# Loading a KV cache in 64 KB rows through one ring of ten units, on one Trainium2 core

## The chip, the core and the metric

The kernel runs on one core of a Trainium2 chip. The core has a matrix engine (TensorE, "PE" in the profile; "PEld" is its loading of weights), a vector engine (DVE), a scalar engine (ACT), a general engine (POOL) and a sync engine (SP), which here only issues DMAs and waits for semaphores. Sixteen DMA engines move data from the memory of the chip (HBM, "dram" in names) to the core's SBUF, which has 128 partitions. PE accumulates into a second memory, PSUM. The metric is the device time of one execution in microseconds.

Each engine runs its own list of instructions in order, and engines meet at semaphores: `wait_ge(s, n)` holds an engine's list until semaphore `s` has reached `n`. A DMA adds 16 to its semaphore, one for each of the sixteen DMA engines that took part, so it counts as landed when the last of them is done.

## The reference

One token passes through an attention block that reads a long KV cache, and through a small gated MLP; a gate mixes the two. Everything is bf16.

```python
H, Sk, Dh, D, F = 32, 65536, 128, 512, 1792
q = (x @ wq).reshape(H, Dh)                                   # x: [1, 512], wq: [512, 4096]
p = softmax(einsum("hd,hkd->hk", q, k_cache) * Dh ** -0.5)    # k_cache: [32, 65536, 128]
a = einsum("hk,hkd->hd", p, v_cache).reshape(1, H * Dh) @ wo  # wo: [4096, 512]
b = (silu(x @ w_gate) * (x @ w_up)) @ w_down                  # [512, 1792] twice, [1792, 512]
g = sigmoid(sum(x * gate_w))
out = g * a + (1 - g) * b
```

K and V are 512 MB each in this count of 1 MB = 2^20 bytes (the profile's MB are 10^6 bytes: 1087.67 with the weights). Each is read once, and there is next to no reuse.

## The kernel before, in words

**Units and tiles.** A head's K is cut into eight chunks of 8192 positions, 2 MB each; so is its V. A chunk fills one 16 KB slot of all 128 partitions: partition p gets 64 consecutive positions, one contiguous row of 16 KB in HBM (`kv_src`, line 145). There are 256 K chunks and 256 V chunks.

**K chunk, on DVE and PE.** DVE transposes the chunk in 32x32 blocks of 32-bit words from the ring into one of two buffers `kt` (line 269, semaphore `ktdone`), which frees the ring slot. PE then multiplies it with the head's query, spread out in `qd`: 64 small matmuls into `psS` (line 346, `qkdone`).

**Head turn.** After a head's eight K chunks DVE takes the maximum of the scores in each partition (line 275), POOL makes it one maximum over all partitions (line 201) and the bias of the exponential (line 203), ACT computes the exponentials and their sum (line 217, `expdone`), and DVE shuffles the result into `pb`, the layout that V needs, in sixteen copies (line 285, `s_pb`). These steps stand in DVE's list among the transposes of the next head: the maximum behind its first chunk, the shuffle behind its second.

**V chunk, on PE alone.** 64 matmuls accumulate a head's output in `psO` straight from the ring (line 363, `pvdone`), which frees the slot. After a head's last V chunk DVE normalises (line 292, `s_otn`) and PE projects the head with its slice of `wo` into `psY` (line 372). One projection stands in PE's list for each head, some chunks later.

**The order of the loads.** `ring_order` (lines 47 to 53) alternates K chunk j with V chunk j - 10, so ten K chunks come first and ten V chunks last. SP issues all loads in that order on one queue; slot n % 7 of the ring is used again when its last user is done (line 185). PE's list has the same order. The weights have tiles of their own, some of which share SBUF space with tiles of other stages: `wq` is loaded first (behind the two small rows of x and gate_w), `w_gate`, `w_up` and `w_down` after two K chunks, `wo` before the thirteenth ring load and after a wait for the MLP (line 181). In HBM, `wq` is read in rows of 8 KB, `w_gate` and `w_up` in 3.5 KB, `w_down` and `wo` in 1 KB.

**MLP.** PE does its first part behind the fourth K chunk (`mlp_up`, line 319) and the second behind the fifth (`mlp_down`, line 328); DVE's part (`mlp_steps`, line 252) stands behind the fifth transpose and holds DVE until PE's second part is done (line 259).

Of the kernel before, what the change touches and what calls it, by code (L numbers as in the profile page):

```python
# [5 lines left out]
P = 128  # L6
CK = 8192
RB = CK // P
NR = RB // 4
NS = 7  # L10
LAG = 10

ALU = mybir.AluOpType
# [3 lines left out]
U32 = mybir.dt.uint32  # L17
AX_X = mybir.AxisListType.X
RMAX = bass.bass_isa.ReduceOp.max
RADD = bass.bass_isa.ReduceOp.add  # L20


def bass_gated_mix__mha_block_cached__swiglu_ffn__decode_kernel(
# [18 lines left out]
    NCH = S // CK  # L42
    NT = H * NCH
    SCALE = float(Dh) ** -0.5
    assert Dh == 128 and D == 512 and F % P == 0 and NCH * RB == 512

    ring_order = []
    for j in range(NT):
        ring_order.append(("k", j))
        if j >= LAG:  # L50
            ring_order.append(("v", j - LAG))
    for j in range(NT - LAG, NT):
        ring_order.append(("v", j))
    slot = {}
    fill = {}
    for n, key in enumerate(ring_order):
        slot[key] = n % NS
        fill[key] = 16 * (n // NS + 1)

    with ExitStack() as ctx:  # L60
# [15 lines left out]

        sel = sb("sel", [P, 4, 128], BF16)
# [21 lines left out]
        ring = sb("ring", [P, NS, RB * Dh], BF16)  # L99

        s_x = sem("s_x")
        s_wq = sem("s_wq")
        s_w1 = sem("s_w1")
        s_wo = sem("s_wo")
        rs = [sem(f"rs{i}") for i in range(NS)]
# [33 lines left out]
        wq_dram = A_wq.rearrange("(c p) n -> p c n", p=P)  # L139
        wg_dram = B_w_gate.rearrange("(c p) f -> p c f", p=P)  # L140
        wu_dram = B_w_up.rearrange("(c p) f -> p c f", p=P)
        wd_dram = B_w_down.rearrange("(c p) n -> p c n", p=P)
        wo_dram = A_wo.rearrange("(h d) n -> d h n", d=Dh)

        def kv_src(kind, j):
            src = A_k_cache if kind == "k" else A_v_cache
            h, c = j // NCH, j % NCH
            return src[0, h, c * CK:(c + 1) * CK, :].rearrange("(p r) d -> p (r d)", p=P)

        with ExitStack() as early:  # L150
            wq_t = early.enter_context(nc.sbuf_tensor("wq_t", [P, Dc, H * Dh], BF16))
            wq_end = nc.sbuf_base
        kt = ctx.enter_context(nc.sbuf_tensor("kt", [P, 2, RB * Dh // 2], U32))
        assert nc.sbuf_base >= wq_end
        with ExitStack() as mlp:
            wg_t = mlp.enter_context(nc.sbuf_tensor("wg_t", [P, Dc, F], BF16))
            wu_t = mlp.enter_context(nc.sbuf_tensor("wu_t", [P, Dc, F], BF16))
            wd_t = mlp.enter_context(nc.sbuf_tensor("wd_t", [P, FC, D], BF16))
            mlp_end = nc.sbuf_base
        wo_t = ctx.enter_context(nc.sbuf_tensor("wo_t", [P, H, D], BF16))  # L160
        if nc.sbuf_base < mlp_end:
            ctx.enter_context(nc.sbuf_tensor("mlp_pad", [P, (mlp_end - nc.sbuf_base + 64) // 2], BF16))

        ktb = [kt[:, b, :].bitcast(BF16).rearrange("p (j r m e) -> p j r m e", j=2, r=NR, e=2) for b in range(2)]

        block = ctx.enter_context(nc.Block())
        MLP_AT = 2
        WO_AT = 12

        @block.sync  # L170
        def _(sp):
            sp.dma_start(xrow[0:1, :], xr_dram).then_inc(s_x, 16)
            sp.dma_start(gwrow[0:1, :], gw_dram).then_inc(s_x, 16)
            sp.dma_start(wq_t[:], wq_dram).then_inc(s_wq, 16)
            for n, (kind, j) in enumerate(ring_order):
                if n == MLP_AT:
                    sp.dma_start(wg_t[:], wg_dram).then_inc(s_w1, 16)
                    sp.dma_start(wu_t[:], wu_dram).then_inc(s_w1, 16)  # L178
                    sp.dma_start(wd_t[:], wd_dram).then_inc(s_w1, 16)  # L179
                if n == WO_AT:  # L180
                    sp.wait_ge(s_b, 1)
                    sp.dma_start(wo_t[:], wo_dram).then_inc(s_wo, 16)
                if n >= NS:
                    pkind, pj = ring_order[n - NS]
                    sp.wait_ge(ktdone if pkind == "k" else pvdone, pj + 1)
                sl = slot[(kind, j)]
                sp.dma_start(ring[:, sl, :], kv_src(kind, j)).then_inc(rs[sl], 16)  # L187
# [20 lines left out]
        def _(act):  # L208
# [12 lines left out]
            act.wait_ge(s_out, 16)  # L221

        @block.vector
        def _(dve):
# [37 lines left out]
            for i in range(NT + LAG + 16):  # L262
                if i < NT:
                    dve.wait_ge(rs[slot[("k", i)]], fill[("k", i)])
                    if i >= 2:
                        dve.wait_ge(qkdone, i - 1)
                    o = kt[:, i % 2, :].rearrange("p (j r t) -> p r j t", j=2, t=32)
                    src = ring[:, slot[("k", i)], :].bitcast(U32).rearrange("p (r j t) -> p r j t", j=2, t=32)
                    nc.vector.transpose(o, src).then_inc(ktdone, 1)  # L269
                if i == 4:  # L270
                    mlp_steps()
                if i % NCH == 0 and 0 <= i // NCH - 1 < H:
                    h = i // NCH - 1
                    dve.wait_ge(qkdone, NCH * (h + 1))
                    nc.vector.reduce_max(mxs[:, h:h + 1], psS[:, h % 2, :], AX_X).then_inc(s_mx, 1)  # L275
                if i % NCH == 1 and 0 <= i // NCH - 1 < H:
                    h = i // NCH - 1
                    dve.wait_ge(expdone, h + 1)
                    if h >= 2:
                        dve.wait_ge(pvdone, NCH * (h - 1))  # L280
                    for g in range(4):
                        for b in range(4):
                            dst = pb[32 * g:32 * g + 32, h % 2, :].rearrange("p (n b) -> p n b", b=4)[:, :, b]
                            sr = pa[32 * b:32 * b + 32, h % 2, :].rearrange("p (n g) -> p n g", g=4)[:, :, g]
                            last = nc.vector.tensor_copy(dst, sr)  # L285
                    last.then_inc(s_pb, 1)
                if i % NCH == 3 and 0 <= i // NCH - 2 < H:
                    h = i // NCH - 2
                    dve.wait_ge(s_L, h + 1)
                    link(nc.vector.reciprocal(Li[:, h:h + 1], Lt[:, h:h + 1]))  # L290
                    dve.wait_ge(pvdone, NCH * (h + 1))
                    nc.vector.tensor_scalar(oTn[:, h:h + 1], psO[:, h % 2, h:h + 1], Li[:, h:h + 1], None,  # L292
                                            ALU.mult).then_inc(s_otn, 1)
# [5 lines left out]
        def _(pe):  # L299
            pe.wait_ge(s_x, 32)  # L300
            pe.wait_ge(s_ones, 1)
            for c in range(Dc):
                last = nc.tensor.matmul(psM[:, c:c + 1], xrow[0:1, c * P:(c + 1) * P], ones1[0:1, 0:1],
                                        start=True, stop=True)
            last.then_inc(s_xT, 1)
            pe.wait_ge(s_xTb, 1)
            pe.wait_ge(s_wq, 16)
            for h in range(H):
                for c in range(Dc):
                    last = nc.tensor.matmul(psM[:, 128 + h:129 + h], wq_t[:, c, h * Dh:(h + 1) * Dh],  # L310
                                            xTb[:, c:c + 1], start=(c == 0), stop=(c == Dc - 1))
# [7 lines left out]
            def mlp_up():  # L319
                pe.wait_ge(s_w1, 48)  # L320
                for fc in range(FC):
                    for w, o in ((wg_t, 64), (wu_t, 80)):
                        for c in range(Dc):
                            last = nc.tensor.matmul(psM[:, o + fc:o + fc + 1], w[:, c, fc * P:(fc + 1) * P],  # L324
                                                    xTb[:, c:c + 1], start=(c == 0), stop=(c == Dc - 1))
                last.then_inc(s_h, 1)

            def mlp_down():
                pe.wait_ge(s_gu, 1)
                for fc in range(FC):  # L330
                    last = nc.tensor.matmul(psB[0:1, :], guT[:, fc:fc + 1], wd_t[:, fc, :],  # L331
                                            start=(fc == 0), stop=(fc == FC - 1))
                last.then_inc(s_b, 1)

            for i in range(NT + LAG + 16):
                if i < NT:
                    h, c = i // NCH, i % NCH
                    pe.wait_ge(ktdone, i + 1)
                    if i == 0:
                        pe.wait_ge(s_qd, 1)  # L340
                    if c == 0 and h >= 2:
                        pe.wait_ge(expdone, h - 1)
                    for r in range(NR):
                        col = c * RB + 4 * r
# [5 lines left out]
                if i == 3:  # L350
                    mlp_up()
                if i == 4:
                    mlp_down()
                if 0 <= i - LAG < NT:
                    v = i - LAG
                    h, c = v // NCH, v % NCH
                    if c == 0:
# [46 lines left out]
```

## Time and profile before

| | |
|---|---|
| median of three runs | 2604.55 us (2604.51 to 2605.13) |
| the profiled execution | 2604.43 us, of which its span, first to last instruction, 2602.6 us |
| HBM read | 1087.64 MB, 418 GB/s over the span |
| DMA, busy share of the sixteen engines | 99.1% for the queue of the loads, 0.7% for instructions |
| DVE transposes of K, line 269 | 256, 1137.5 us busy |
| PE on K, line 346, and on V, line 363 | 16384 matmuls each, 478.2 and 472.8 us busy |
| K and V DMAs from issue to landing, median | 31.2 and 29.9 us |

A row of the timeline has a start and a duration in us from the span's start, the engine, the line of the kernel, the operation, output and inputs, and how often; in brackets stands how long the engine had been idle before, and what ended that. "issue" means that the engine waited for nothing that the profile shows. A row of the windows has a stretch, its length, the busy time and the number of instructions of PE, PEld, DVE, ACT and POOL, then the granted clock of PE, the busy share of the sixteen DMA engines and the rate of all transfers. Besides these the trace holds one record for every DMA packet (queue, start, duration, size) and one for every DMA engine's landing of every DMA.

### The profile page before, as it was taken

To read this page: it belongs to the slowest core of one execution; us is meant where nothing else is said; L and a number is where in the kernel's file an instruction comes from. 1 tells how busy PE (TensorE), PEld (TensorE's weight loads), DVE (VectorE), ACT (ScalarE), POOL (GpSimd) and SP (SyncE) were. 2 spreads that over 40 slices of the span, in tenths; PEclk is the share of its full clock that TensorE was granted. 3 is DMA by queue.
4 is the path that set the end of the run, shared out by engine and by line. 5 is a ranking of instruction groups with operands and counts; after the bars stand their busy time and mean duration, and the time that the engine had idled before them with its cause. 6 is when DMAs were issued, how large, how long until landed. Compare 5 with 4: busy or idle time off the path is not lost.

```text
span 2602.6 us, 68273 instructions
## 1 busy us (share of the span) xinstructions
PE 946.4 (36%) x33062; PEld 906.0 (35%) x33062; DVE 1324.6 (51%) x883; ACT 26.6 (1%) x67; POOL 34.7 (1%) x105
## 2 busy tenths in 40 slices
PE   2333333333333333333333333333333333333334
PEld 2333333333333333333333333333333333333333
DVE  4655454554455554555545555455555454554451
ACT  0000000000000000000000000000000000000000
POOL 0000000000000000000000000000000000000000
PEclk9555555555555555555555555555555555555555
DMA  9999999999999999999999999999999999999997
GB/s 397 412 426 426 426 425 426 426 426 427 425 426 426 425 425 427 425 423 419 426 421 423 420 421 423 425 421 420 421 420 425 422 420 425 415 426 423 420 420 309
DMA packets 81512, 1092.03 MB, mean 420 GB/s; under 512 B 8275, under 2 KB 14166, under 8 KB 15190
## 3 DMA queue, kind: packets, MB, share of 16 engines
q1 hardware_dynamic: 81236, 1087.67, 99.1%
q8 instruction: 258, 4.23, 0.7%
q14 instruction: 16, 0.13, 0.0%
q10 hardware_dynamic: 2, 0.00, 0.0%
HBM read 1087.64 MB, written 0.00 MB: 418 GB/s over the span
## 4 chain that ended last, share of the span: by engine, by line
DMA 76%; DVE 12%; PE 9%; issue 1%; SPq 1%; ACT 0%; POOL 0%; POOLq 0%; DVEq 0%
DMA ring<-in_A_k_cache_dram 75%; DVE kt L269 11%; PE psS L346 5%; PE psO L363 4%; DMA ring<-in_A_v_cache_dram 1%; SPq L179 1%; SPq L187 0%; DVE pb L285 0%; PE psB L331 0%; PE psM L324 0%; SPq L178 0%; ACT pa L217 0%; DVE mxs L275 0%; DVE brow L260 0%; POOL amx L201 0%
## 5 line engine op out<-in xcount | busy, mean ns | idle before, releaser
L269 DVE STREAM_TRANSPOSE kt<-ring 128x4096 uint32<-128x4096 uint32 x256 | 1137.5, 4445 | 1142.6 <-DMA ring<-in_A_k_cache_dram 1141.5
L346 PE MATMUL psS<-qd,kt 128*128 128x4 bf16 x16384 | 478.2, 166 | 1606.3 <-DVE kt L269 1606.3
L346 PEld LDWEIGHTS psS<-qd,kt 128*128 128x128 bf16 x16384 | 457.0, 104 | 1640.6 <-DVE kt L269 1640.6
L363 PE MATMUL psO<-pb,ring 128*128 128x1 bf16 x16384 | 472.8, 165 | 30.8 <-DMA ring<-in_A_v_cache_dram 22.7
L363 PEld LDWEIGHTS psO<-pb,ring 128*128 128x128 bf16 x16384 | 456.8, 104 | 32.2 <-DMA ring<-in_A_v_cache_dram 23.8
L285 DVE COPY pb<-pa 32x128 bf16<-32x128 bf16 x512 | 154.5, 302 | 71.3 <-ACT pa L217 64.7
L217 ACT ACTIVATE pa<-psS,nbias 128x512 bf16<-128x512 f32 x32 | 22.0, 687 | 2475.1 <-POOL nbias L203 2475.1
L201 POOL PARTITION_ALL_REDUCE amx<-mxs x32 | 11.8, 368 | 1945.2 <-DVE mxs L275 1945.2
L292 DVE TENSOR_SCALAR oTn<-psO,Li 128x1 bf16<-128x1 f32 x32 | 7.1, 222 | 30.1 <-PE psO L363 29.1
L275 DVE TENSOR_REDUCE mxs<-psS 128x1 f32<-128x512 f32 x32 | 20.9, 653 | 2.0 <-PE psS L346 2.0
L372 PE MATMUL psY<-wo_t,oTn 128*1 128x512 bf16 x32 | 18.8, 587 | 0.4 <-DVE oTn L292 0.4
L205 POOL PARTITION_ALL_REDUCE Lt<-rsum x32 | 12.8, 400 | 285.6 <-issue 285.6
L203 POOL TENSOR_SCALAR nbias<-amx 128x1 f32<-128x1 f32 x32 | 8.3, 260 | 294.4 <-issue 294.4
L310 PE MATMUL psM<-xTb,wq_t 128*128 128x1 bf16 x128 | 3.5, 165 | 11.5 <-DMA wq_t<-in_A_wq_dram 11.5
L310 PEld LDWEIGHTS psM<-xTb,wq_t 128*128 128x128 bf16 x128 | 3.5, 104 | 11.6 <-issue 11.6
L245 DVE CAST qTb<-psM 128x32 bf16<-128x32 f32 x1 | 0.2, 192 | 14.0 <-PE psM L310 14.0
L217 ACT ACTIVATION_READ_ACCUMULATOR pa<-psS,nbias 128x1 f32 x32 | 6.2, 193 | 0.0
L290 DVE RECIPROCAL Li<-Lt 128x1 f32<-128x1 f32 x32 | 4.0, 123 | 3.9 <-POOL Lt L205 3.9
L331 PE MATMUL psB<-wd_t,guT 128*1 128x512 bf16 x14 | 5.9, 613 | 0.0
L260 DVE TENSOR_SCALAR brow<-psB,sc 1x512 f32<-1x512 f32 x1 | 0.7, 737 | 6.5 <-PE psB L331 6.5
L324 PE MATMUL psM<-xTb,wu_t 128*128 128x1 bf16 x56 | 3.2, 165 | 2.1 <-issue 2.1
L324 PEld LDWEIGHTS psM<-xTb,wu_t 128*128 128x128 bf16 x56 | 2.7, 104 | 2.1 <-issue 2.1
(31 smaller groups left out, 19.3 us busy)
## 6 DMA issues: line engine op xcount, KB each, us to landing
ring<-in_A_k_cache_dram SPq DMA_DIRECT2D x256, 2048.0 KB, 31.2
ring<-in_A_v_cache_dram SPq DMA_DIRECT2D x256, 2048.0 KB, 29.9
wq_t<-in_A_wq_dram SPq DMA_DIRECT2D x1, 4096.0 KB, 12.7
wo_t<-in_A_wo_dram SPq DMA_DIRECT2D x1, 4096.0 KB, 32.0
wg_t<-in_B_w_gate_dram SPq DMA_DIRECT2D x1, 1792.0 KB, 26.5
wu_t<-in_B_w_up_dram SPq DMA_DIRECT2D x1, 1792.0 KB, 30.3
wd_t<-in_B_w_down_dram SPq DMA_DIRECT2D x1, 1792.0 KB, 33.8
xrow<-in_A_x_dram SPq DMA_DIRECT2D x1, 1.0 KB
```

The costliest lines, as they stand in the source:

```text
L179: sp.dma_start(wd_t[:], wd_dram).then_inc(s_w1, 16)
L201: nc.gpsimd.partition_all_reduce(amx[:, h:h + 1], mxs[:, h:h + 1], P, RMAX).then_inc(s_ar, 1)
L203: nc.gpsimd.tensor_scalar_mul(nbias[:, h:h + 1], amx[:, h:h + 1], -SCALE).then_inc(s_nb, 1)
L205: nc.gpsimd.partition_all_reduce(Lt[:, h:h + 1], rsum[:, h:h + 1], P, RADD).then_inc(s_L, 1)
L217: nc.scalar.activation(pa[:, h % 2, :], psS[:, h % 2, :], ACT.Exp, bias=nbias[:, h:h + 1], scale=SCALE, accum_out=rsum[:, h:h + 1]).then_i ...
L269: nc.vector.transpose(o, src).then_inc(ktdone, 1)
L275: nc.vector.reduce_max(mxs[:, h:h + 1], psS[:, h % 2, :], AX_X).then_inc(s_mx, 1)
L285: last = nc.vector.tensor_copy(dst, sr)
L292: nc.vector.tensor_scalar(oTn[:, h:h + 1], psO[:, h % 2, h:h + 1], Li[:, h:h + 1], None, ALU.mult).then_inc(s_otn, 1)
L346: last = nc.tensor.matmul(psS[:, h % 2, col:col + 4], ktb[i % 2][:, je // 2, r, :, je % 2], qd[:, h, je, :], start=(je == 0), stop=(je == 3))
L363: last = nc.tensor.matmul(psO[:, h % 2, h:h + 1], ring[:, slot[("v", v)], r * Dh:(r + 1) * Dh], pb[:, h % 2, c * RB + r:c * RB + r + 1], s ...
L372: last = nc.tensor.matmul(psY[0:1, :], oTn[:, h:h + 1], wo_t[:, h, :], start=(h == 0), stop=(h == H - 1))
```

## The change

The ring becomes one circle of ten units of 16 KB a partition (`RING`, `UNIT`), and it is the only place for loads: `wq` takes two units, `w_gate`, `w_up` and `w_down` one each, `wo` two, and they free them as K and V do.

K and V are loaded four units at a time (`ROW`): one DMA of 8 MB whose rows, one for each partition, are 64 KB long in HBM, so partition p has 256 consecutive positions. A group that would cross the end of the circle is split there into two DMAs. Work on a unit, its matmuls and its transpose, is as before.

`plan_stream` writes the order: `wq`, the first K group, the three MLP weights, then K groups; from the fifth K group on (`lag` is four groups), each K group is followed by one V group. After the last K group come the remaining V groups, `wo` just before the last head's V, and that head's second half in pieces of 2, 1 and 1 units. x and gate_w are issued after `wq`. PE's list follows the same order, group by group. A DMA waits for the last users of all the units that it overwrites, and its landing is counted on one of twelve semaphores in turn.

The rows of `wq`, `w_gate`, `w_up` and `w_down` are dealt to the partitions contiguously (`(p c)` for `(c p)`), which makes rows of 32, 14, 14 and 14 KB; `mlp_up` and the transposition of x read with a stride to fit. `wo` keeps rows of 1 KB.

The normalisation of a head stands three heads later in DVE's list, those of the last three heads at the end. The projections leave the loop: those of the first 31 heads stand in one run behind the fourth V unit of the last head, the last one at the end.

```diff
-CK = 8192
-RB = CK // P
-NS = 7
-LAG = 10
+PC = 64
+UNIT = PC * 128
+RING = 10
+ROW = 4
+NSEM = 12
...
+def plan_stream(H, NP):
+    per = NP // ROW
+    ks = [("k", h, u * ROW, ROW) for h in range(H) for u in range(per)]
+    vs = [("v", h, u * ROW, ROW) for h in range(H - 1) for u in range(per)]
+    vs += [("v", H - 1, 0, 4), ("v", H - 1, 4, 2), ("v", H - 1, 6, 1), ("v", H - 1, 7, 1)]
+    lag = 2 * per
+    items = [("wq", 0, 0, 2)]
+    n = 0
+    for i, it in enumerate(ks):
+        items.append(it)
+        if i == 0:
+            items += [("wg", 0, 0, 1), ("wu", 0, 0, 1), ("wd", 0, 0, 1), ("pad", 0, 0, 1)]
+        if i >= lag:
+            items.append(vs[n])
+            n += 1
+    while n < len(vs):
+        if vs[n] == ("v", H - 1, 0, 4):
+            items.append(("wo", 0, 0, 2))
+        items.append(vs[n])
+        n += 1
+    return items
...
+    for kind, h, u0, nu in items:
+        done = 0
+        while done < nu:
+            k = min(nu - done, RING - pos % RING)
+            slots = [(pos + j) % RING for j in range(k)]
+            if kind != "pad":
+                waits = [owner[s] for s in slots if owner[s] is not None]
+                n = len(dmas)
+                dmas.append((kind, h, u0 + done, k, slots[0], waits))
...
+            pos += k
+            done += k
...
-        wq_dram = A_wq.rearrange("(c p) n -> p c n", p=P)
-        wd_dram = B_w_down.rearrange("(c p) n -> p c n", p=P)
+            "wq": A_wq.rearrange("(p c) n -> p (c n)", c=Dc),
+            "wd": B_w_down.rearrange("(p c) n -> p (c n)", c=FC),
...
+            for n, (kind, h, u0, k, s0, waits) in enumerate(dmas):
+                need = {}
...
+                for w, s in (("wq", s_q), ("wg", s_h), ("wu", s_h), ("wd", s_b), ("k", ktdone), ("v", pvdone)):
+                    if w in need:
+                        sp.wait_ge(s, need[w])
+                dst = ring[:, s0 * UNIT:(s0 + k) * UNIT]
+                if kind in "kv":
+                    cache = A_k_cache if kind == "k" else A_v_cache
+                    src = cache[0, h].rearrange("(b p r) d -> b p (r d)", p=P, r=ROW * PC)[
+                        u0 // ROW, :, (u0 % ROW) * UNIT:(u0 % ROW + k) * UNIT]
...
+                sp.dma_start(dst, src).then_inc(ds[n % NSEM], 16)
...
+            for i, (h, u) in enumerate(kunits):
+                arrived(dve, ("k", h, u))
+                if i >= 2:
+                    dve.wait_ge(qkdone, i - 1)
...
+                nc.vector.transpose(o, src).then_inc(ktdone, 1)
                 if i == 4:
                     mlp_steps()
+                if u == 0 and h >= 1:
+                    head_max(h - 1)
+                if u == 1 and h >= 1:
+                    head_shuffle(h - 1)
+                if u == 4 and h >= 3:
+                    head_norm(h - 3)
...
+            for kind, h, u0, nu in items:
+                for u in range(u0, u0 + nu):
+                    if kind == "k":
+                        i = kseq[(kind, h, u)]
+                        pe.wait_ge(ktdone, i + 1)
...
+                    elif kind == "v":
...
+                        arrived(pe, (kind, h, u))
...
+                        last.then_inc(pvdone, 1)
+                        if h == H - 1 and u == 3:
+                            arrived(pe, ("wo", 0, 0))
+                            for hh in range(H - 1):
+                                project(hh)
+            project(H - 1)
```

## The prediction

> **What bounds the kernel now.** I read the page first: shares of the span, DMA queues, the chain that ended last. All sixteen DMA engines are busy from end to end and the chain is made of transfers; no compute engine is above 51%.
>
> ```profile
> span 2602.6 us, 68273 instructions
> ...
> PE 946.4 (36%) x33062; PEld 906.0 (35%) x33062; DVE 1324.6 (51%) x883; ACT 26.6 (1%) x67; POOL 34.7 (1%) x105
> ...
> q1 hardware_dynamic: 81236, 1087.67, 99.1%
> q8 instruction: 258, 4.23, 0.7%
> ...
> DMA 76%; DVE 12%; PE 9%; issue 1%; SPq 1%; ACT 0%; POOL 0%; POOLq 0%; DVEq 0%
> ```
>
> Then the windows of the last stage (stretch, length, PE, PEld, DVE, ACT, POOL busy, clock, DMA share, GB/s):
>
> ```profile
> 2540.00:2550.00 10.00, 3.78 (x142) 3.70 (x139) 5.14 (x2) 0.00 (x0) 0.37 (x1) 0.50 1.00 423
> ...
> 2580.00:2585.00 5.00, 1.87 (x64) 1.78 (x64) 0.00 (x0) 0.00 (x0) 0.00 (x0) 0.50 0.50 213
> ```
>
> For the last 20 us half of the DMA engines work: eight lag. The landing records (one per DMA engine) say the same: the sixteen landings of one 2 MB DMA lie 3.5 us apart at 141 us, 22 us at 1099 us, and no further later. The landings of successive DMAs stand 4.992 us apart throughout. A DMA counts when its slowest engine is done, so the lagging eight set the pace, and they lag because the 258 instruction packets of q8 go to eight engines in turn: such a packet takes 1.06 us, and the 16 KB packet behind it 1.15 us instead of 0.61. That is 1.6 us for each of 32 fetches, 52 us on each slow engine.
>
> Last, the timeline, for prices that the new order needs (start, length, what):
>
> ```profile
> 57.55 0.17 PE L324 MATMUL psM<-xTb,wu_t 128*128 128x1 bf16 x1
> ...
> 59.77 0.22 PE L324 MATMUL psM<-xTb,wu_t 128*128 128x1 bf16 x3 [2.05 <-issue]
> ...
> 62.27 5.93 PE L331 MATMUL psB<-wd_t,guT 128*1 128x512 bf16 x14
> ...
> 69.00 17.42 DVE L269 STREAM_TRANSPOSE kt<-ring 128x4096 uint32<-128x4096 uint32 x4
> ...
> 86.35 0.65 DVE L275 TENSOR_REDUCE mxs<-psS 128x1 f32<-128x512 f32 x1
> ...
> 95.87 5.01 DVE L285 COPY pb<-pa 32x128 bf16<-32x128 bf16 x16 [4.52 <-ACT pa L217]
> ...
> 2597.43 1.86 PE L363 MATMUL psO<-pb,ring 128*128 128x1 bf16 x64 [3.01 <-DMA ring<-in_A_v_cache_dram]
> ```
>
> A transpose of one unit takes 4.35 us in a row, a V or QK unit 1.87 us of PE, a 512-wide projection 0.425 us (14 in 5.93), the head shuffle 5.0. From a head's maximum to its shuffle pass 8.9 to 12.9 us, mean 10.8 (POOL and ACT). PE stops where its instructions run out: counted by its instructions, a fetch is asked for every 256, its packet starts 1.8 us plus up to one 16 KB packet later (mean 2.15), and PE resumes about 1.4 after it ends, 4.6 us after the request, while 180 instructions (2.6 us) are in hand. Hence the 2.05 us at 57.7.
>
> **The change, part by part.** The profiled execution took 2604.43 us, 1.83 around its span of 2602.6, and 0.1 below the median of 2604.55; the sum stands against it.
>
> *Rows of 64 KB.* An engine moves 4096 packets of 16 KB for K and V. Their records, undisturbed, last 614.1 ns and overlap by 3.6: a step of 610.5. The 8 KB packets step by 306.8, the 1 KB ones by 47.2. So a packet costs beyond its bytes: 3.1 ns from 8 and 16 KB (2 x 306.8 - 610.5), 9.6 from 1 and 16 KB. Every fourth descriptor lasts 7 ns longer, which points to a cost per descriptor. I take 4 ns, near the larger rows. After, 1024 rows of 64 KB; where a group crosses the circle's end (every fifth, some 26 in all) it goes as two pieces, 1248 packets with the small last ones. 2848 fewer x 4 = **-11.4** (-8.8 to -27.3). Could a long row be slower? The slowest undisturbed 16 KB packets (624 ns) four in a row give 2482 a row against 2442, +41 us: the outer bound. Some 355 fewer DMAs drop 16 semaphore packets each, 5.4 ns per engine: **-1.9**.
>
> *Weights in contiguous rows.* wd falls from 112 rows of 1 KB per engine to 7 of 14 KB, wg and wu from 64 to 16, wq from 32 to 8; at 9.6, 8.8 and 3.1 ns **-1.4**; wo keeps its 1 KB rows and moves from the start to before the last V groups: the same transfer elsewhere, and SP's wait for the MLP ahead of it (9.4 us, hidden by seven queued DMAs) goes. mlp_up now reads weights 28 bytes apart. No row shows that stride; kt's 4-byte stride costs no more than contiguous (104 ns both). At 104 ns unoverlapped for 112 loads, 12 us instead of 3.3, K's third group is issued 3 us late; bound 0 to +3, taken as 0. x and gate_w now queue behind wq and land near 12 us instead of 2; q follows by 20 us, hidden by the first K group's landing at 31.
>
> *The start.* Now 8 MB land at once and four units must be emptied one by one. A DMA is issued when its four slots are free: those of the last two units of the group three before it and of the first two of the group two before. A group takes 19.45 us to land. Transfers, back to back: wq to 11.4, K0 to 30.9, wg, wu and wd to 43.7, K1 to 63.1, K2 to 82.6, K3 to 102.0, K4 to 121.5 (their slots come free 1 to 5 us ahead). DVE empties K0 by 49, waits for K1 and has its first unit at 67.9; the MLP steps hold it to 76.6 (PE's 5.95 among them, with all later transposes queued behind). K1 is done at 89.7, K2's first two units and the maximum at 99.0, the shuffle (9.0 after the maximum in this stage) from 103.6 to 108.6, K2 at 117.3, K3's second unit at 126.0. V0 needs that one: its data flow at 127.7 (1 us from issue, and 0.65 more for first packets, as where engines ran dry at 1541 us), **6.2 late**. K4's last unit follows at 162.5, its QK at 164.4. V1 needs V0's second unit, which PE takes only then: a fetch of 5.5 (below), 1.1, and 1.65 make 172.7, due at 166.5, **6.1 late**. While SP waits here, the K groups behind it wait too, but their slots are no earlier. The kernel before lost about 1 to stalls here. **+11** (5 to 18).
>
> *Every head.* With T the landing of a head's first K group: units at T+4.4 and 9.4, shuffle to 20.9, last unit 29.6, its QK 31.5. Only then does PE take the V group landed at T+20, whose first two units free the slots of the V group after next; that must flow from T+39.3. PE's requests fall at the end of every second unit (the count of the preamble is 18 beyond a multiple of 256, a unit has 128 instructions, and this stays so), so one falls where this QK ends. It waits 1.8 us plus part of a row that now lasts 2.43, so it arrives after 4.3 to 6.7, 5.5 in the mean; PE has 1.1 of the two units left then, and the data flow 1.65 later: T+39.4 on average, against T+39.3. With 9.3 us from maximum to shuffle, as in the first half of the trace, nothing is late; with 12, as in the second, 1.3. Where the K or the V group is cut by the circle's end there are 10 us more, which leaves 17 of 30 heads: 17 x 1.3 = 22 were all like the second half, 0 like the first. **+6** (0 to 25), the lower half, since the long waits came with the lag of 22 us, for which this order leaves no room. In the kernel before SP was far ahead here: a K DMA landed 31 us after its issue.
>
> *The end.* Now one V unit, 1.87, follows the last landing E; then 3.3 of normalisation, projection and output in both. After, projections of 31 heads wait for the last head's first V group (E - 19.5). From there PE does 4 x 1.87, a fetch stall of 2.3, 31 x 0.425 = 13.2, 4 x 1.87, a short fetch 0.8: 31.3, so E + 11.8 against E + 1.9. **+10** (7 to 14).
>
> Sum: -11.4 - 1.9 - 1.4 + 11 + 6 + 10 = +12.3; 2604.4 + 12.3 = **2617**, slower by 0.5%.
>
> A row against a rule: the queue moves 426 GB/s with 2 MB DMAs back to back. The Trainium skill ("DMA: Bandwidth & Descriptors", Bandwidth, Measured) has 341 GB/s at 1 MB and 425 at 16 MB, measured from GpSimd; from 383 (their mean, for 2 MB) to 425 the estimate would be 1088 MB in 2.56 ms instead of 2.84, 280 us gained. The trace has no such gap to close. Against the change the same page (Latency and other measured facts) warns of row pitches at powers of two: 207 GB/s at 512 KB against 214 padded. At that 3% the estimate would be some 80 us lost; no row here has a 64 KB pitch.
>
> **Rivals.** *Faster, 2595.* One mechanism: the descriptor cost is that of the small rows (9.6 ns, 27.3 instead of 11.4), and fetches get in between the pieces of a row, so heads don't stall (6 less). It decides from about 8 ns a packet on. For it: 1 KB and 3.5 KB packets agree (9.6, 8.8). Against: these lie in the disturbed first 100 us, the 8 KB ones don't fit.
> *Heads stall, 2640 to 2670.* A fetch waits for more than one row: 2.4 to 3.6 us later, 17 tight turns at 1.5 to 3 more, the same once each at start and end. For it: the slack is nil by my sum. Against: today's delay spreads by one packet only.
> *The rows are cut again to 16 KB:* no gain of 11.4, but no long wait either: 2622.
> *No change, 2601:* DVE's backlog and the projections cost half of what I take (10 less) and heads don't stall (6 less). For it: the start is worked out over five landings, each uncertain by 1 us. Against: the projections' 13.2 us come from a row of their own kind.
>
> **How the numbers follow.** Forecast 0.50 (own range 2608 to 2628), faster 0.15, heads stall 0.15, cut rows 0.07, no change 0.13. A difference under 0.2% (5.2 us) can't be told. Faster 0.15; same 0.13 and a little of the forecast's low edge, 0.16; slower 0.69. The range 2598 to 2650 leaves out most of the faster case, the upper half of the stalls and rows near the outer bound.
>
> **What would show it.** K and V packets of 64 KB lasting about 2430 ns (2415 is the rival); GB/s falling short of the pace near 125 and 170 us; SP issuing V groups just as the queue runs dry; PE idle with "issue" of 2 to 4 us inside V groups; 31 projections in one run of 13 us, ending some 8 us before the last PV unit; the last landing to the end 15 us instead of 5. The prediction is wrong if rows take more than 2450 ns, or if landings in mid-run stand further apart than 19.9 us per 8 MB.

## The result: slower by 1.0%

The changed kernel takes 2631.47 us (median of five runs, 2628.02 to 2636.45) against 2604.55 us (2604.19 to 2605.13). The ratio is 1.0102, with a 95% interval of 1.0087 to 1.0117. The direction was the one forecast, the size was not: +27 us instead of +12. The profiled execution took 2628.02 us, 23.6 more than the one profiled before; the accounts below are between these two.

The page after, from its first lines to the chain:

```profile
span 2626.2 us, 68015 instructions
...
GB/s 414 374 383 427 430 395 412 427 395 432 426 402 406 421 431 397 427 411 403 430 433 411 428 409 419 433 427 417 433 422 420 435 429 412 431 418 421 428 428 334
...
q1 hardware_dynamic: 27012, 1087.65, 97.1%
q8 instruction: 258, 4.23, 0.6%
...
DMA 63%; issue 16%; DVE 15%; PE 6%; POOL 0%; ACT 0%; SPq 0%; POOLq 0%; DVEq 0%
```

The rate has two faces. Some slices run at 430 to 435 GB/s, above anything in the kernel before (427 at most), others fall to 374 to 411. The number of packets fell to a third, the share of the queue from 99.1 to 97.1%: faster transfers with holes between them. In the chain, "issue" and DVE have taken a part that was DMA's.

The windows show where a hole is (columns as before):

```profile
80.00:120.00 40.00, 10.23 (x354) 9.82 (x355) 32.98 (x25) 0.78 (x2) 0.71 (x3) 0.53 0.98 414
120.00:160.00 40.00, 14.03 (x484) 13.36 (x481) 31.90 (x15) 0.78 (x2) 0.97 (x3) 0.50 0.81 338
160.00:200.00 40.00, 18.28 (x640) 17.68 (x640) 29.03 (x16) 0.00 (x0) 0.40 (x1) 0.50 0.87 367
```

These are the two late V groups of the start, V0 and V1. In SP's list V0 is issued at 132.0 us, while the group before it landed at 127.1; V1 at 177.2, the group before at 174.8. One later head, from the timeline of the kernel after:

```profile
542.66 4.45 DVE L333 STREAM_TRANSPOSE kt<-ring 128x4096 uint32<-128x4096 uint32 x1 [21.65 <-DMA ring<-in_A_k_cache_dram]
547.03 0.65 DVE L307 TENSOR_REDUCE mxs<-psS 128x1 f32<-128x512 f32 x1
547.61 4.42 DVE L333 STREAM_TRANSPOSE kt<-ring 128x4096 uint32<-128x4096 uint32 x1
...
560.22 0.26 POOL L244 TENSOR_SCALAR nbias<-amx 128x1 f32<-128x1 f32 x1 [12.06 <-issue]
...
561.32 5.02 DVE L317 COPY pb<-pa 32x128 bf16<-32x128 bf16 x16 [9.29 <-ACT pa L258]
566.38 8.77 DVE L333 STREAM_TRANSPOSE kt<-ring 128x4096 uint32<-128x4096 uint32 x2
...
575.20 1.87 PE L409 MATMUL psS<-qd,kt 128*128 128x4 bf16 x64 [2.46 <-DVE kt L333]
...
576.93 2.27 PE L425 MATMUL psO<-pb,ring 128*128 128x1 bf16 x80
581.27 4.88 PE L425 MATMUL psO<-pb,ring 128*128 128x1 bf16 x176 [2.06 <-issue]
...
582.76 0.33 SPq L225 DMA_DIRECT2D ring<-in_A_v_cache_dram  x1
```

A K group landed at 542.66. DVE empties two of its units, waits 9.3 us for the exponentials, shuffles, and only then empties the other two (566.4 to 575.2). PE comes to the V group behind them at 576.9, stops 2.06 us for instructions, and SP can issue at 582.8. The transfer in flight had landed at 581.3.

An account at equal amounts of K and V landed, from the landing records of the two profiled executions (`wo` is loaded at opposite ends of the two streams; its own time, 12.0 us in the landings before and 11.6 after, is taken out of both and has a row of its own):

| stretch | after less before, us |
|---|---|
| up to 36 of 512 units | +11.0 |
| units 36 to 300 | +14.6 |
| units 300 to 504 | -3.0 |
| the last 8 units | -0.1 |
| `wo` itself | -0.4 |
| last landing to the end (6.8 against 5.2) | +1.6 |

In the first half V groups come late and the change loses; in the second half they do so less, and it gains a little. By the late shuffle below, 8 us go to waiting even there.

### The profile page after: what moved, and what is told of

It reads as the page before. It is cut to its first block, busy times and chain, and to the rows that moved or that the text cites. A ratio compares the mean times of both kernels' runs of the same rounds, so it can differ in the third digit from the quotient of the medians.

```text
span 2626.2 us, 68015 instructions
## 1 busy us (share of the span) xinstructions
PE 956.2 (36%) x33062; PEld 917.7 (35%) x33062; DVE 1308.1 (50%) x883; ACT 26.6 (1%) x67; POOL 34.9 (1%) x105
## 3 DMA queue, kind: packets, MB, share of 16 engines
q1 hardware_dynamic: 27012, 1087.65, 97.1%
## 4 chain that ended last, share of the span: by engine, by line
DMA 63%; issue 16%; DVE 15%; PE 6%; POOL 0%; ACT 0%; SPq 0%; POOLq 0%; DVEq 0%
DMA ring<-in_A_k_cache_dram 59%; DVE kt L333 12%; DMA ring<-in_A_v_cache_dram 4%; PE psO L425 4%; DVE pb L317 2%; PE psS L409 1%; DVE mxs L307 1%; PE psY L391 0%; PE psB L385 0%; POOL amx L242 0%; POOL nbias L244 0%; ACT pa L258 0%; DVE Li L322 0%; DVE oTn L324 0%; POOLq L244 0%
## 5 line engine op out<-in xcount | busy, mean ns | idle before, releaser
L333 DVE STREAM_TRANSPOSE kt<-ring 128x4096 uint32<-128x4096 uint32 x256 | 1126.0, 4426 | 946.3 <-DMA ring<-in_A_k_cache_dram 910.6
L425 PE MATMUL psO<-pb,ring 128*128 128x1 bf16 x16384 | 458.9, 165 | 336.6 <-issue 221.7
L425 PEld LDWEIGHTS psO<-pb,ring 128*128 128x128 bf16 x16384 | 448.9, 104 | 344.6 <-issue 259.2
L244 POOL TENSOR_SCALAR nbias<-amx 128x1 f32<-128x1 f32 x32 | 8.3, 261 | 344.9 <-issue 344.9
L391 PE MATMUL psY<-ring,oTn 128*1 128x512 bf16 x32 | 9.4, 457 | 0.4 <-DVE oTn L324 0.4
L278 DVE CUSTOM_DVE_ANT_0 xg<-xrow,gwrow 1x512 f32<-1x512 bf16 x1 | 0.7, 678 | 12.4 <-DMA gwrow<-in_gate_w_dram 12.4
L377 PE MATMUL psM<-xTb,ring 128*128 128x1 bf16 x112 | 6.9, 198 | 0.0
L377 PEld LDWEIGHTS psM<-xTb,ring 128*128 128x128 bf16 x112 | 6.8, 158 | 0.0
L385 PE MATMUL psB<-ring,guT 128*1 128x512 bf16 x14 | 5.5, 573 | 0.0
```

Of the source, the lines that this page charges most:

```text
L244: nc.gpsimd.tensor_scalar_mul(nbias[:, h:h + 1], amx[:, h:h + 1], -SCALE).then_inc(s_nb, 1)
L377: last = nc.tensor.matmul(psM[:, o + j:o + j + 1], w[:, c, :, j], xTb[:, c:c + 1], start=(c == 0), stop=(c == Dc - 1))
L391: last = nc.tensor.matmul(psY[0:1, :], oTn[:, h:h + 1], wo_ap[:, h, :], start=(h == 0), stop=(h == H - 1))
L425: last = nc.tensor.matmul(psO[:, h % 2, h:h + 1], vt[:, r * Dh:(r + 1) * Dh], pb[:, h % 2, u * PC + r:u * PC + r + 1], start=(u == 0 and r ...
```

## Seven experiments

**Late shuffle.** DVE's shuffle moves from behind the second transpose of the next head to behind the seventh.

```diff
-                if u == 1 and h >= 1:
+                if u == 6 and h >= 1:
                     head_shuffle(h - 1)
```

> The kernel after, with one edit: DVE shuffles a head's exponentials behind the seventh transpose of the next head instead of behind the second, so that it no longer holds transposes 3 and 4 back while POOL and ACT work. Theory A (the head turn on DVE, 12.4 us from maximum to shuffle and 5 us of copies, keeps ring slots from coming free in time, so the DMA queue runs dry at the 17 heads whose groups are not cut by the ring's end, some 33 us in all, and once at the start): no late V group is left, some 33 us less at the heads and 5 to 10 less at the start, 2580 to 2592 us, below the kernel before. Rival B (64 KB rows or 8 MB DMAs are themselves slow, the late issues only coincide): 2620 to 2632.

2579.81 us; against the kernel before, 0.9905 (0.989 to 0.9919). One moved line takes 51.7 us off the changed kernel (48.4 between the profiled executions) and puts it 24.7 below the one before. The same place in the timeline:

```profile
522.82 4.45 DVE L333 STREAM_TRANSPOSE kt<-ring 128x4096 uint32<-128x4096 uint32 x1 [16.75 <-DMA ring<-in_A_k_cache_dram]
...
527.77 13.07 DVE L333 STREAM_TRANSPOSE kt<-ring 128x4096 uint32<-128x4096 uint32 x3
...
540.90 1.87 PE L409 MATMUL psS<-qd,kt 128*128 128x4 bf16 x64 [2.46 <-DVE kt L333]
...
547.41 3.55 PE L425 MATMUL psO<-pb,ring 128*128 128x1 bf16 x128 [2.50 <-issue]
...
548.90 0.33 SPq L225 DMA_DIRECT2D ring<-in_A_v_cache_dram  x1
```

From a landing of K to the issue of the V group pass 26.1 us instead of 40.1. PE still stops 2.5 us for instructions, now with room to spare. No DMA of the run is issued after the one before it has landed, and the windows of the start are full:

```profile
120.00:160.00 40.00, 17.30 (x613) 16.74 (x611) 30.73 (x23) 0.78 (x2) 1.43 (x4) 0.50 0.99 415
160.00:200.00 40.00, 15.57 (x550) 15.06 (x547) 25.26 (x21) 0.00 (x0) 0.00 (x0) 0.50 0.99 424
```

By the account above, the late shuffle is 13.2 us better up to unit 36, 27.8 from there to 300 and 8.1 to 504. So the head turn cost 36 us and the start 13. Theory A holds, and rival B is out: the rows and the DMAs are those of the change, and the kernel is 24.7 us faster than the one before.

**Fetch phase.** 64 unused matmuls shift PE's requests for instructions by one unit.

```diff
             last.then_inc(s_qs, 1)
+            for _ in range(64):
+                nc.tensor.matmul(psM[:, 300:301], sel[:, 0, :], qTb[:, 0:1], start=True, stop=True)
```

> The kernel after, with 64 unused matmuls (128 PE instructions, 1.9 us, in a stretch where PE waits for K) behind the query's spreading, which moves PE's requests for instructions by one unit: they fall behind the third K unit of a group and not behind the fourth. Theory A (in the first half of the run a stall of some 2 us for instructions inside the first two V units makes the next V group late; in the second half the request has drifted clear of it): 8 heads and one group of the start about 2.1 us sooner, 2608 to 2616 us. Rival B (the stall for instructions lies beside the wait for DMA and costs nothing): 2626 to 2632.

2625.73 us (2621.42 to 2632.84), 1.0084 (1.0067 to 1.0101): less gained than expected. Two heads of this kernel, one in each half of the run:

```profile
573.76 0.56 PE L427 MATMUL psO<-pb,ring 128*128 128x1 bf16 x16
574.55 4.61 PE L427 MATMUL psO<-pb,ring 128*128 128x1 bf16 x166 [0.22 <-issue]
577.75 0.33 SPq L225 DMA_DIRECT2D ring<-in_A_v_cache_dram  x1
...
2170.13 3.44 PE L427 MATMUL psO<-pb,ring 128*128 128x1 bf16 x124
...
2176.16 2.00 PE L427 MATMUL psO<-pb,ring 128*128 128x1 bf16 x70 [2.58 <-issue]
...
2176.48 0.33 SPq L225 DMA_DIRECT2D ring<-in_A_v_cache_dram  x1
```

Up to unit 300 the kernel is 14.6 us ahead of the change, as Theory A has it for the heads: no stop of 2 us ahead of the issue. (The start gained nothing; it is 0.4 us later.) Then it loses 8.1 up to unit 504: the request drifts by about two instructions a head (in the change PE gets through 80 V matmuls before the stop at 579 us, and 73 seven heads later), and in the second half the stop moves into the second V unit, where the change had none. Another 5.2 go at the end (12.0 us from last landing to the end instead of 6.8), where PE now stops twice for 3 us in the last head's first V group. So a stop inside the first two V units does make the next V group late; that a shift would help the whole run was wrong.

**A DMA for every unit.** Order, ring and layout stay, rows of 16 KB at a distance of 64 KB.

```diff
-            k = min(nu - done, RING - pos % RING)
+            k = 1 if kind in "kv" else min(nu - done, RING - pos % RING)
```

> The kernel after, order, ring and layout the same, but every K and V unit has a DMA of its own: 2 MB in rows of 16 KB that lie 64 KB apart in HBM. Theory A (the late issues come from freeing and landing in 8 MB; a 64 KB packet is worth 24 ns against four of 16 KB, 24 us over the run): the head stalls of 33 us go, half of the 11 at the start too, 24 us for shorter rows and 2 for semaphore packets come back, 2608 to 2620 us. Rival B (the layout, rows 64 KB apart, makes reading slow): 2640 or more, with longer packets.

2601.26 us, 0.9987 (0.9977 to 0.9996), better than expected: with 2 MB landings no DMA is issued after the one before it has landed, the start included, and the shuffle stands where the change has it. Rows 64 KB apart read at the old rate (undisturbed packets of 614 ns), so rival B is out. POOL's wait between the maximum and the bias, by line 244 of the waits (in total, times, longest), is also shorter than in the change:

```profile
POOL nbias L244 <- issue: 293.5, 32, 11.2
```

The change has 344.9 there, 10.8 a head against 9.2.

**More instruction packets, in the kernel before.** 64 unused matmuls behind every V chunk.

```diff
                     last.then_inc(pvdone, 1)
+                    for _ in range(64):
+                        nc.tensor.matmul(psM[:, 300:301], sel[:, 0, :], qTb[:, 0:1], start=True, stop=True)
```

> The kernel before, with 64 unused matmuls behind each V chunk on PE: 32768 more PE instructions, so 128 more instruction packets, 16 on each of the eight DMA engines that carry them; PE has the time for it. Theory A (each instruction packet costs its engine 1.6 us and the eight engines that carry them set the pace): 16 x 1.6 = 26 us more, 2626 to 2634 us, landings 5.04 us apart instead of 4.99. Rival B (the packets are hidden, eight engines lag for another reason): 2604 to 2607 us.

2637.2 us, 1.0125 (1.011 to 1.014): +32.7 us.

```profile
span 2635.3 us, 101041 instructions
...
q8 instruction: 386, 6.32, 1.0%
```

```profile
2622.00:2635.00 13.00, 10.57 (x360) 9.89 (x360) 0.96 (x2) 0.00 (x0) 0.00 (x0) 0.50 0.02 4
```

Two things make up the 32.7 us. The last landing comes at 2621.7 us instead of 2597.4: 24.3 us by the transfers. After it PE is still at work for 13 us, as the row of the windows shows (DMA 0.02), because the added matmuls and their stops put it behind at the end: 13.6 us from the last landing to the end instead of 5.2, 8.4 us that are no cost of DMA. The expectation had PE's time for nothing there, and its range is missed by that part. The 24.3 us are 1.5 us for each of the 16 more packets of an engine; landings in mid-run stand 5.04 us apart instead of 4.99, and eight engines are 22 us behind by 800 us instead of 1100. Theory A holds, with its price of 1.6.

**The rows alone.** Late shuffle and a DMA for every unit together (both edits above).

> The kernel with the late shuffle and, besides, a DMA of its own for every unit (16 KB rows, 64 KB apart). With no head stall in either, it differs from the late shuffle by the rows alone. Theory A (the 16 KB packet steps by 610.5 ns, the 64 KB packet by 2414 to 2420, 22 to 28 ns a row, 23 to 28 us over the 1024 rows of an engine, 2 us of semaphore packets): 2602 to 2610 us. Rival B (the value of long rows is what was forecast, 4 ns for each packet saved, 11 us): 2591 to 2595 us.

2599.47 us, 0.9981 (0.9971 to 0.999): between the two theories. Against the late shuffle these are 19.7 us, but the late shuffle loses 2.4 of its gain after its last landing (7.6 us to the end, where this kernel has 5.2). By the last landings the difference is 22.5 us, and 22.6 in the times of this kernel and of the early projections below, whose end is 5.2 us too. Some 2 of it are semaphore packets; 20.5 us for 2848 packets are 7.2 ns each. Undisturbed records would give more: a 64 KB row lasts 2420 ns (overlapping by 3.6) where four 16 KB packets step by 2442, 25 us over an engine's rows, those of 32 KB included. A part is given back: what packets last beyond their median, summed and divided by sixteen, is 31.5 us with long rows and 19.2 with short ones. That mean over all engines is 12 us apart and would leave 13 of the 25; the landings go by the slowest engines, and their share was not separated. Against the unit DMAs with the early shuffle the place of the shuffle is worth 1.8 us, where it was worth 51.7 with 8 MB groups.

**Half the group.** Groups of two units, 32 KB rows.

```diff
-ROW = 4
+ROW = 2
...
-    vs += [("v", H - 1, 0, 4), ("v", H - 1, 4, 2), ("v", H - 1, 6, 1), ("v", H - 1, 7, 1)]
+    vs += [("v", H - 1, 0, 2), ("v", H - 1, 2, 2), ("v", H - 1, 4, 2), ("v", H - 1, 6, 1), ("v", H - 1, 7, 1)]
...
-        if vs[n] == ("v", H - 1, 0, 4):
+        if vs[n] == ("v", H - 1, 0, 2):
```

> The kernel after with groups of two units instead of four: DMAs of 4 MB in rows of 32 KB, shuffle behind the second transpose as in the change. Theory A (the stall comes from a ring of 2.5 groups: with five groups of half the size, slots come free two units at a time and several groups ahead): no V group late at a head; a 32 KB packet lasts 1213 ns, two of them 8 to 10 ns more than one of 64 KB, 8 to 10 us over the run: 2583 to 2595 us. Rival B (the head turn on DVE stalls the queue whatever the size of the groups): 2615 or more.

2583.31 us, 0.9917 (0.9901 to 0.9934). The shuffle is where the change has it and no V group is late; the rate of the page is even:

```profile
GB/s 411 418 428 428 429 428 430 428 427 430 428 430 428 428 429 427 429 431 427 429 422 430 427 427 427 425 426 429 426 426 428 423 428 425 416 429 423 430 399 310
```

POOL's wait is as long as in the change (10.7 a head), so it is not the wait alone that stalls the queue, but the wait together with a ring of two and a half groups.

**Early projections.** Late shuffle, and the 31 projections ahead of the last head's V instead of behind its fourth unit.

```diff
                     elif kind == "v":
+                        if h == H - 1 and u == 0:
+                            arrived(pe, ("wo", 0, 0))
+                            for hh in range(H - 1):
+                                project(hh)
...
-                        if h == H - 1 and u == 3:
-                            arrived(pe, ("wo", 0, 0))
-                            for hh in range(H - 1):
-                                project(hh)
```

> The kernel with the late shuffle, and the 31 projections put ahead of the last head's V, into the 20 us in which PE waits for its landing (PE idle 22.4 us there). Theory A (the end costs what PE still has to do after the last landing; 7.6 us from the last landing to the end, 5.2 in the kernel before): 5.0 to 5.5 us from landing to end, 2576 to 2579 us. Rival B (PE slows down without the long run of projections, which had raised its clock, and gives it back): 2579 to 2582 us.

2576.87 us, 0.9893 (0.9879 to 0.9908), the fastest version: 27.7 us below the kernel before and 54.6 below the change. From the last landing to the end pass 5.2 us again.

## Why the prediction was right in direction and wrong in size

**Every head, forecast +6 (0 to 25): this is the step that failed; 36 us.** Place, chain and the number of tight heads were right (17, all of them V groups where nothing is cut by the ring's end); the slack was not.

- The wait from maximum to shuffle was taken too short. It was 13.6 us in the head shown above and 12.4 on average, where 10.8 was used and 9.3 thought likely for half the run. The longer part is POOL's. The forecast took the lower half of its range because the long waits had come with the lag of 22 us. That reason failed: after the change the sixteen landings of a DMA never lie more than 5.7 us apart, and the first sixteen heads still wait 12.3 us on average.
- The forecast's own sum was short. Its terms 31.5, 5.5, 1.1 and 1.65 make T+39.75 and not T+39.4, so by them a head was late by 0.45 us and not by 0.1.
- The time by which the data had to flow was a little late: T+39.3 in the forecast, while the group in flight landed 38.7 us after T. Faster rows are some 0.2 us of that, an estimate from sixteen rows of an engine at a step of 2416 ns for 2430.

With 12.4 for 10.8 the same terms give T+41.35, 2.05 us late at 17 heads, 35 us. That the total fits is in part luck: 28 of the 36 us fell into the first half and 8 into the second, since the stop for instructions drifts, which the forecast had as staying in place ("this stays so"). The fetch was named as the last term, and it is one: in the first half it was worth 14.6 us, as the fetch phase shows. And +6 was the low side of an expectation about zero slack, where every further microsecond counts 17 times. One of the forecast's own signs of being wrong came about: up to unit 300 the landings stand 20.2 us apart per 8 MB, over its limit of 19.9. The whole is nearer to the forecast than this term, by luck: the rows came out 9 us better than forecast and the end 8.

**Rows, forecast -11.4 (-8.8 to -27.3): 20.5 gained by the rows alone**, 7.2 ns a packet for 4. The size was off and the bound held. The undisturbed records (2418 to 2420 ns a packet) are near the sign of the rival with 9.6 ns (2415). Of the weights' rows no run shows the price; the forecast's terms for them add up to -1.5, not -1.4.

**Start, forecast +11: right.** 13 us against the late shuffle, in V0 and V1, with the same causes. All of it lies some 5 us later than in the forecast; 3 of them were there when the first K group landed, at 33.9 us instead of 31. mlp_up with its stride of 28 bytes took 6.9 us instead of 3.3, inside the bounds; with the late shuffle the same reads stand in a start without a late group, so they cost nothing there.

**End, forecast +10 (7 to 14): +1.6.** The run of 31 projections took 8.8 us, not 13.2. After, at the end:

```profile
2605.56 2.09 PE L425 MATMUL psO<-pb,ring 128*128 128x1 bf16 x73 [1.97 <-issue]
...
2607.58 8.78 PE L391 MATMUL psY<-ring,oTn 128*1 128x512 bf16 x31
...
2616.29 6.63 PE L425 MATMUL psO<-pb,ring 128*128 128x1 bf16 x256
```

And in the windows the granted clock doubles in the middle of it:

```profile
2608.00:2612.00 4.00, 4.00 (x12) 1.26 (x11) 0.00 (x0) 0.00 (x0) 0.00 (x0) 0.56 1.03 434
2612.00:2616.00 4.00, 4.00 (x21) 1.51 (x18) 0.00 (x0) 0.00 (x0) 0.00 (x0) 1.00 0.65 279
2616.00:2624.00 8.00, 7.50 (x259) 6.63 (x257) 0.29 (x2) 0.00 (x0) 0.00 (x0) 0.86 0.05 18
```

The first ten projections take 0.43 us each, the other 21 about 0.22: the clock rose 3.9 us into their run (3.5 to 5.1 us in the other kernels that have such a run). The Trainium skill says this ("TensorE: Matmul & The Clock Gate", Part 1: The HAM clock gate (the "warmup" mystery)): some 3.4 us of sustained activity release the gate, and idling closes it. For the projections, 512 columns wide, the trace agrees. For V's matmuls, one column wide, it does not. A burst of 256 of them in a head of the second half, 7.15 us without a stop, left the clock at 0.50:

```profile
2182.30 7.15 PE L425 MATMUL psO<-pb,ring 128*128 128x1 bf16 x256
```

And at the end the clock falls back at 2621.75 us by the trace's record of it, while the last V units still run without a stop (hence the mean of 0.86 above). Whether the width is the reason was not tried. The price of 0.425 us came from a run of 14 in 6 us and should not have been stretched to 31. The eight V units around the projections took 15.6 us with their stops, forecast 18.0, and the last landing came 21.0 us after that of the last head's first V group, not 19.5.

**Rivals.** "Heads stall" was the right case with the wrong cause in it: POOL was late. Fetches did not wait for two rows: in the head shown PE resumes 4.2 us after its request, where 5.5 was forecast. "Faster, 2595" needed 9.6 ns a packet and no stalls at the heads; with the late shuffle 7.2 ns, heads without stalls and a start without stalls come together, and that kernel is at 2580.

**The two rules that were weighed.** The 280 us estimated from the sizes of DMAs were not there: 8 MB against 2 MB was worth 20.5 us in rows and 2 in semaphores. Nor was the loss from row distances at a power of two: rows of 16 KB that lie 64 KB apart read as fast as contiguous ones, 614 ns both (the page's smallest distance, 512 KB, no run here has).

## What to carry to other kernels

When a ring is loaded in larger pieces, count it in pieces: ten units were five buffers of two and only two and a half of four, and a pause of DVE that was free at 2 MB cost 36 us at 8 MB. Free the ring first and do the slow, waiting step behind it: moving one step in DVE's list was worth more than the longer rows that the change was made of. A forecast whose slack comes out near zero, with a multiplier of 17, has no central value; its range is what the terms' spread makes of it.

## What was not expected of the hardware

Instruction fetches are a load on the DMA engines: 258 packets of 16 KB, 0.4% of the bytes, cost 1.5 us each on eight engines that set the pace, by the 24.3 us of 128 more. For 32 packets an engine this makes an estimated 49 us of a run of 2604. The Trainium skill ("Runtime: NRT & Kernel Launch", Instruction fetch mechanics) gives blocks of 256 instructions, which the traces show exactly, and calls the crossing mostly hidden; here it is not, neither for the DMA engines nor for PE, which stops for 2 to 3 us inside a long burst of V (2.06, 2.50 and 2.58 us in the rows above).

POOL's wait between the all-reduce and the bias differs with the loads, though POOL issues no DMA here: 9.2 to 9.9 us a head with 16 KB packets in the kernels with unit DMAs, 10.5 to 10.9 with 32 and 64 KB. The size of the packets is not all of it. In the kernel before, with 16 KB throughout, the wait rises from a mean of 7.8 us over the first 14 heads to 10.3 over the rest, from when the lagging DMA engines have fallen 22 us behind; with the rows alone it rises from 9.2 to 11.7 after the first 23 heads. The cause was not tried and stays open, as does the reason why disturbed packets cost 12 us more with long rows.
